# Column sums of phi(K) taken in the gram products, two row tiles turned by TensorE, and the whole program's order, engines and banks read from tables

## The chip, the cores and the metric

The kernel runs on one core of a Trainium2 chip. A time is the device time of one launch in microseconds (us); the time of a kernel is the median of its runs. The engines of the core are named as the profile names them: PE (TensorE, with PEld for its weight loads), DVE (VectorE), ACT (ScalarE), POOL (GpSimd) and SP (SyncE, which here only issues DMAs).

## The reference

Two kinds of layer alternate, each twice, on x of 2048 rows and 512 columns. The same weights serve both rounds.

```python
def _A_ref(x, wqkv, wo):          # H = 32 heads of 16
    q, k, v = split(x @ wqkv)
    phi = lambda t: jnp.where(t > 0, t + 1, jnp.exp(t)) + 1e-6
    pq, pk = phi(q), phi(k)
    kv = jnp.einsum("bhsd,bhse->bhde", pk, v)
    z = jnp.einsum("bhsd->bhd", pk)
    num = jnp.einsum("bhqd,bhde->bhqe", pq, kv)
    den = jnp.einsum("bhqd,bhd->bhq", pq, z)[..., None] + 1e-6
    return merge_heads(num / den) @ wo

def _B_ref(x, w1, w3, w2):        # F = 1792
    return (_silu(x @ w1) * (x @ w3)) @ w2

x = x + _A_ref(_layernorm(x), A_wqkv, A_wo)
x = x + _B_ref(_layernorm(x), B_w1, B_w3, B_w2)
x = x + _A_ref(_layernorm(x), A_wqkv, A_wo)
x = x + _B_ref(_layernorm(x), B_w1, B_w3, B_w2)
```

z is the sum of phi(K) over all 2048 rows, one number for each of the 512 columns.

## The kernel before

**Precision.** Each float32 operand of a product is scaled by a power of two and held as two float16 parts, high and low. A product takes three passes on PE: low by high, high by high, high by low (`PASSES`, L32; `mm`, L494). Splitting an operand costs a high part (a copy or a scaled copy to float16) and a low part (a subtraction, with two inputs).

**A pair of layers** is traced by `pair` (L1435): `attention` (L862), then `mlp` (L1444). `layer` 0 and 1 are the two rounds.

**Attention, keys.** The rows are cut into 16 tiles of 128. A tile is normalised (`keys_rows`), split into `nat` (two parts of 512 columns), turned by a DMA transpose into `xt` (`keys_turn`, L1107; the first three tiles by `ln_tile`, L484), and multiplied by the key weights: 12 matmuls of 512 columns into the PSUM tile `pk`. `phi_act` and `phi_sum` make phi(K), `high` and `low` (L914, L928) split it. `gram` (L878) adds nat-transposed times phi(K) into four banks `gt`, 12 matmuls a tile. The products with V's weights come later: `kv_products` multiplies the whole gram by them.

**Column sums before.** In layer 0 `gram_sum` (L870) multiplies both parts of phi(K) by a matrix of ones, two matmuls of 512 columns a tile, into the bank `pz`. In layer 1 POOL adds the tiles into `pksum` (L916 to L920), and `totals` (L953) sums over the partitions with one float32 matmul. Either way `pz` then holds z in every row, `inverse`, `keep_z`, `columns` (L981, eight float32 matmuls of one column) use it.

**Queries.** For each tile a product `pq` (`query`, L1148), phi, a denominator (`weigh_in`, `weigh_out`), a split and a DMA transpose, a product `po` with the combined weights `m_s`, and the sum into x (`attn_add`, L1209).

**MLP.** One level of a seven-product scheme: a group (`mlp_group`, L1287) has seven products P1 to P7 of 12 matmuls of 256 columns, for gate and up together, into the banks `ba`, `bb`, `bc`. ACT copies `bb` out between them (L1310), DVE adds `ba` and `bc` (L1313), then Silu on ACT (L1265), the product with up on DVE (L1266), the split of the hidden values (`hidden_parts`, L1268: high on ACT L1269, low on DVE or POOL L1271), four sums for the scheme (L1281 to L1284), and `mlp_out` (L1345, matmuls L1357; or `mlp_out_plain`, L1366) two groups later, into banks `po`. `mlp_add` (L1389) adds the banks into x. The columns of F come in seven groups in two or three sets, the rows in four chunks.

**Background in layer 0.** The MLP weights are loaded, bounded, split and stored while layer 0 runs: by `fill` inside attention and by `steps` inside the MLP.

**Order before.** Inside `in_order` (L257) each engine runs in the order in which the program is traced: the head and both attentions. The MLPs are ordered by the scheduler of the language, with `later` (L165) shifting priorities. PSUM is two pools of four banks, `acc` and `w`. Which engine takes a movable operation stands partly in the strings of `ENGINES` (L183; letter V is DVE, P is POOL, A is ACT), and partly in the code: normalising, the high parts of weights and hidden values, and the copies out of `bb` are always ACT's.

**Queues.** All DMAs go through SP in one queue, transposes too.

**Head.** 22 matmuls on ones keep PE busy, then the bound of the key weights, 10 more, the split of the key weights and the first three tiles.

Of the kernel before, what the change touches and what calls it, by code (L numbers as in the profile page):

```python
# [17 lines left out]
P = 128  # L18
# [9 lines left out]

SX = 2.0**9
PASSES = ((0, 0), (1, 0), (0, 1))  # L32

# [34 lines left out]
AT_JUNK = AT_T + 4 * KB  # L68
XB0, XB1 = AT_XB, AT_XB + 14 * KB


class Ring:
# [5 lines left out]
    def next(self, dtype, *dims):  # L78
        at = self.offsets[self.n % len(self.offsets)]
        self.n += 1  # L80
        return self.view(at, dtype, *dims)

# [6 lines left out]
def kernel(  # L89
# [15 lines left out]
    small = ctx.enter_context(tc.tile_pool(name="small", bufs=4))  # L105
    psum = ctx.enter_context(tc.tile_pool(name="psum", bufs=4, space=PSUM))
    dram = ctx.enter_context(tc.tile_pool(name="dram", bufs=1, space=DRAM))

    arena = const.tile([P, AT_END // 4], F32, name="arena")
# [17 lines left out]
    def acc_bank(name):  # L127
        return psum.tile([P, 512], F32, tag="acc", name=name)

    def bank(name):  # L130
        return psum.tile([P, 512], F32, tag="w", name=name)

    nats = (span(XB1 + 8 * KB, 3), span(AT_W2 + 2 * GROUP2, 3))
    nat_ring = Ring(view, *span(AT_NAT, 3), *nats[0])
# [30 lines left out]
    def later(n):  # L165

        return tc.high_priority(offset=-n)

    PINNED = ("PE", "DVE", "Activation", "Pool", "SP")
# [14 lines left out]
        (  # L184
            "plain:YYNN hid:VPVVVPVVVVVVVVPPVVVVVVVVVVVV den:AVVVVVVVVVVAVAAA "
            "bq:VAAA nat:PPAPAPPPAPPAAAAA key:PPPPPPAAPAAAAPPA "
            "norm:VVVPPPPPPPVVVVVV w13:PPPVVVV w2:PPVVPPP "
            "sums:VVVVVVVVVVVVVVVVVVPPPPPVPVVP rowsum:PPVVVVPP rowlow:PPVVVVVV "
            "keylow:PPPPPPPVVVPPPPPP natlow:PPPPPPPPPPPPPPPP "
            "add:PPPPPPVVVPPPVPPVPPPPVPVP"  # L190
        ),
        (
            "plain:NNNNNNNY hid:VVVVVVVVVVVVVVVVVVVVVVVVVVVV den:VVVVVVVVVVVVVVVV "
            "nat:AAAPPPPAPPPPPAAA key:AAAAAAPPAAAPPPAA "
            "norm:VVVPVVVPPVVVVVPP sums:VVVVVVVPVVVPPPPVVVVVVPVPVVVV "
            "rowsum:PPPPPPPP rowlow:PPPPPPPP keylow:PPPPPPPPPPPPPPPP "
            "natlow:PPPPPPPPPPPPPPPP add:PPPPPPPPPPPPPPPPPPPPPPPP"
        ),
# [57 lines left out]
    @contextmanager  # L256
    def in_order(*engines):  # L257

        traced = nc.cur_bb.bb.instructions
        before = traced[-1]  # L260
        depth.append(engines)
        yield
        depth.pop()
        if depth:
            return
        start = next(k for k in reversed(range(len(traced))) if traced[k] is before) + 1
        for i in traced[start:]:
            if str(i.engine).split(".")[-1] not in (engines or PINNED):
                continue
            if i.engine in pinned:  # L270
                tc.add_manual_dep(
                    i,
                    pinned[i.engine].name,
                    mybir.DependencyInfo(
                        mybir.DependencyClass.NoSync, mybir.DependencyReason.DATA
                    ),
                    reason="in_order",
                )
            pinned[i.engine] = i


    ident = view(AT_UV + 2 * KB, F32, P)
    make_identity(nc, ident)
    ones = const.tile([P, P], F32, name="ones")
    nc.vector.memset(ones, 1.0)
# [3 lines left out]
    make_block_diagonal(nc, mask, DH)  # L289
    scalars = const.tile([P, 42], F32, name="scalars")  # L290
    column = iter(range(38))

    columns_ = scalars[:, 38:42]
# [7 lines left out]
    nc.vector.memset(one_row[:1], 1.0)  # L301
    small_eps = scalar()
# [27 lines left out]
    st_w13 = view(AT_W + 42 * KB, F32, 2, 2, 2, F)  # L330
    raw2_ring = Ring(view, *span(AT_W + 28 * KB, 4))
# [55 lines left out]
    def split(hi, lo, src, scale):  # L387
        nc.scalar.activation(hi, src, AF.Copy, scale=scale)
        nc.vector.scalar_tensor_tensor(lo, src, scale, hi, OP.mult, OP.subtract)
# [8 lines left out]
    def engine_of(what, i):  # L398
        table = {what: table_of(what, state["layer"])}
        return {"V": nc.vector, "P": nc.gpsimd, "A": nc.scalar}[table[what][i]]  # L400
# [7 lines left out]
    def high_part(what, i, dst, src):  # L408
        engine = engine_of(what, i)
        if engine is nc.scalar:  # L410
            engine.activation(dst, src, AF.Copy)
        else:
            engine.tensor_copy(dst, src)

# [4 lines left out]
    def split_late(hi, lo, src, scale):  # L419

        nc.scalar.activation(hi, src, AF.Copy, scale=scale)  # L421
# [11 lines left out]
    def attn_bound(name, i):  # L433
        parts = small.tile([P, NK], F32, tag="parts", name="parts")
# [23 lines left out]
    def ln_moments(t0, n):  # L458
        for t in range(t0, t0 + n):
            st = small.tile([P, 6], F32, tag="st", name="st")  # L460
# [3 lines left out]
    def ln_scale(t0, n):  # L464

        ve = small.tile([P, n], F32, tag="ve", name="ve")
# [4 lines left out]
        neg = small.tile([P, n], F32, tag="neg", name="neg")  # L471
# [3 lines left out]
    def normalise(dst, t):  # L475
        nc.scalar.activation(  # L476
            dst,
            x_sb[:, t, :],
            AF.Identity,
            scale=rs_all[:, t : t + 1],  # L480
# [1248 lines left out]
```

## Time and profile before

| what | us |
|---|---|
| median of 3 runs | 1194.54 |
| lowest and highest run | 1193.79, 1195.58 |
| span of the profiled execution | 1192.4 |

The page gives no time of its own for the profiled execution beside its span; what lies around a span is taken as the median less the span, 2.1 us. The span runs from the first to the last instruction. A busy time is the sum of the durations of an engine's instructions with overlaps counted once; matmuls follow each other faster than one of them lasts, so the time of a matmul in a row is read from the distance of the starts. A line number is one of the kernel before. The row of the page with the DMA's share, in 40 slices of 29.8 us, shows where the queue is full:

```profile
DMA  8966665869632212111316434574342350120000
```

### The profile page before, as it was taken

What the parts mean: (1) busy time and instruction counts of PE and PEld (TensorE: products, weight loads), DVE (VectorE), ACT (ScalarE), POOL (GpSimd) and SP (SyncE); (2) the same over time, 40 slices, a digit from 0 to 9 for tenths busy, and PEclk for the clock granted to TensorE, in tenths of its full rate; (3) what the DMA queues carried; (4) which work ended last, traced back from release to release, by engine and by line L of the source; (5) the groups of instructions that cost most, each with busy time, mean ns of one, the idle gap of its engine ahead of it and who ended that gap; (6) DMA issues with size and microseconds to landing.
All of it is one profiled execution on the core that took longest, in us unless ns stands there. A gap on an engine that the chain in (4) does not pass through costs nothing.

```text
span 1192.4 us, 21837 instructions
## 1 busy us (share of the span) xinstructions
PE 1151.7 (97%) x8884; PEld 867.0 (73%) x8884; DVE 838.8 (70%) x1380; ACT 637.9 (53%) x1068; POOL 433.0 (36%) x500
## 2 busy tenths in 40 slices
PE   8999997899999999999999999998899999999998
PEld 3445444788888878888864454467788888888887
DVE  6888889767878887767785459757765654756443
ACT  6777687756545454434456644675544444444432
POOL 6452577212001121224358824774721122102010
PEclk9999999899999999999999999999999999999999
DMA  8966665869632212111316434574342350120000
GB/s 263 330 228 221 150 144 132 246 216 307 155 142 98 81 61 82 63 63 63 81 51 179 107 100 101 118 164 114 104 115 86 125 186 8 74 80 37 1 36 36
DMA packets 163396, 147.43 MB, mean 124 GB/s; under 512 B 129632, under 2 KB 138976, under 8 KB 158688
## 3 DMA queue, kind: packets, MB, share of 16 engines
q1 hardware_dynamic: 163296, 146.04, 42.1%
q8 instruction: 69, 1.13, 0.4%
q14 instruction: 31, 0.25, 0.1%
HBM read 72.48 MB, written 42.07 MB: 96 GB/s over the span
## 4 chain that ended last, share of the span: by engine, by line
PE 72%; DVE 13%; ACT 5%; DMA 5%; POOL 3%; issue 2%; SPq 1%; DVEq 0%; ACTq 0%; POOLq 0%
PE bb L499 18%; PE po L1357 14%; PE bc L499 9%; PE pq L499 6%; PE gt L499 5%; PE po L499 5%; PE pk L499 5%; PE ba L499 4%; PE po L1377 4%; DMA arena<-arena 3%; DVE arena L1266 2%; DMA arena<-in_B_w_dram 2%; DVE arena L1271 1%; DVE arena L1406 1%; ACT arena L1269 1%
## 5 line engine op out<-in xcount | busy, mean ns | idle before, releaser
L499 PEld LDWEIGHTS <-arena 128*128 128x128 f16 x6360 | 618.2, 98 | 260.9 <-issue 16.1
L499 PE MATMUL bb<-arena 128*128 128x256 f16 x2688 | 331.8, 273 | 7.4 <-ACT arena L1310 5.9
L1357 PE MATMUL po<-arena 128*128 128x256 f16 x1932 | 237.8, 274 | 11.5 <-ACT arena L1269 9.0
L1357 PEld LDWEIGHTS <-arena 128*128 128x128 f16 x1932 | 188.6, 98 | 37.5 <-ACT arena L1269 11.3
L1310 ACT ACTIVATE arena<-bb 128x512 f32<-128x512 f32 x196 | 115.2, 590 | 164.4 <-PE bb L499 135.2
L1271 DVE TENSOR_TENSOR arena<-arena 128x512 f16<-128x512 f32 (+1 forms) x108 | 123.9, 1148 | 96.8 <-ACT arena L1269 96.7
L499 PE MATMUL bc<-arena 128*128 128x256 f16 x1344 | 165.6, 273 | 1.6 <-DVE arena L1313 1.2
L1269 ACT ACTIVATE arena<-arena 128x512 f16<-128x512 f32 (+1 forms) x112 | 99.7, 891 | 95.7 <-DVE arena L1284 39.7
L1426 POOL TENSOR_TENSOR arena<-arena 128x512 f32<-128x512 f32 x28 | 40.4, 1442 | 286.1 <-DVE arena L1406 264.6
L1265 ACT ACTIVATE arena<-arena,scalars 128x512 f32<-128x512 f32 x112 | 74.7, 667 | 102.8 <-DVE arena L1313 100.7
L1266 DVE SCALAR_TENSOR_TENSOR arena<-arena,scalars 128x512 f32<-128x512 f32 x112 | 85.9, 767 | 52.8 <-ACT arena L1265 52.6
L1313 DVE TENSOR_TENSOR arena<-arena,bc 128x512 f32<-128x512 f32 x112 | 76.3, 682 | 50.3 <-ACT arena L1310 45.7
L1406 DVE SCALAR_TENSOR_TENSOR arena<-po,scalars,arena 128x256 f32<-128x256 f32 (+1 forms) x170 | 91.7, 583 | 14.0 <-PE po L1357 11.4
L499 PE MATMUL po<-arena 128*128 128x512 f16 x384 | 87.8, 379 | 4.1 <-DMA arena<-arena 2.8
L499 PE MATMUL pk<-arena 128*128 128x512 f16 x384 | 87.8, 379 | 2.8 <-DMA arena<-arena 2.8
L499 PE MATMUL gt<-arena 128*128 128x512 f16 x384 | 87.8, 379 | 1.6 <-ACT arena L915 1.0
L499 PE MATMUL pq<-arena 128*128 128x512 f16 x384 | 87.4, 379 | 0.9 <-DVE arena L1044 0.9
L499 PE MATMUL ba<-arena 128*128 128x256 f16 x672 | 86.3, 273 | 0.0
L476 ACT ACTIVATE arena<-arena,nb_all,rs_all 128x512 f32<-128x512 f32 x64 | 50.4, 808 | 32.3 <-POOL nb_all L473 28.3
L1377 PE MATMUL po<-arena 128*128 128x256 f16 x480 | 59.7, 280 | 3.4 <-ACT arena L1269 3.4
L423 DVE SCALAR_TENSOR_TENSOR arena<-arena,scalars 128x512 f16<-128x512 f32 (+2 forms) x60 | 50.3, 853 | 15.4 <-ACT arena L421 14.1
L1252 POOL TENSOR_TENSOR arena<-arena 128x512 f16<-128x512 f32 (+2 forms) x30 | 44.0, 1491 | 39.3 <-DMA arena<-arena 37.8
(164 smaller groups left out, 1258.3 us busy)
## 6 DMA issues: line engine op xcount, KB each, us to landing
arena<-xb_d SPq DMA_DIRECT2D x12, 1792.0 KB, 6.8
xb_d<-arena SPq DMA_DIRECT2D x8, 1792.0 KB, 5.9
xt_d<-arena SPq DMA_DIRECT2D x32, 256.0 KB, 2.5
arena<-xt_d SPq DMA_DIRECT2D x32, 256.0 KB, 3.1
arena<-in_B_w_dram SPq DMA_DIRECT2D x8, 896.0 KB, 7.2
arena<-in_B_w_dram SPq DMA_DIRECT2D x28, 256.0 KB, 4.1
w_d<-arena SPq DMA_DIRECT2D x4, 1792.0 KB, 9.5
arena<-w_d SPq DMA_DIRECT2D x4, 1792.0 KB, 6.8
```

What stands on the lines that cost most here:

```text
L423: lambda: nc.vector.scalar_tensor_tensor(lo, src, scale, hi, OP.mult, OP.subtract)
L476: nc.scalar.activation(dst, x_sb[:, t, :], AF.Identity, scale=rs_all[:, t : t + 1], bias=nb_all[:, t : t + 1],)
L499: nc.tensor.matmul(dst, lhs(a, k), rhs(b, k), start=first and k == 0 and i == 0, stop=last and k == n - 1 and i == len(PASSES) - 1, skip_g ...
L1265: nc.scalar.activation(t, gate, AF.Silu, scale=info["u1"])
L1266: nc.vector.scalar_tensor_tensor(t, up, info["hid"], t, OP.mult, OP.mult)
L1269: nc.scalar.activation(hs[:, 0, lo:hi], t[:, lo:hi], AF.Copy)
L1271: engine.tensor_tensor(hs[:, 1, lo:hi], t[:, lo:hi], hs[:, 0, lo:hi], OP.subtract)
L1310: nc.scalar.activation(dst, bank_, AF.Copy)
L1313: nc.vector.tensor_tensor(dst, dst, bank_, OP.add)
L1357: nc.tensor.matmul(po[:, i * HALF : (i + 1) * HALF], hs[:, a, qx, cs], w2[:, b, qw, :], start=g == ends[0] and i + a + b == 0, stop=g == e ...
L1377: nc.tensor.matmul(acc[n][:, half * HALF : (half + 1) * HALF], hs[:, a, qx, cs], w2_a21[g][:, b] if (i, half) == (0, 1) else w2[:, b, i + ...
L1406: nc.vector.scalar_tensor_tensor(dst, src, cb, to, OP.mult, OP.add)
```

## The change

1. **Column of ones.** `nat` of a key tile becomes 1026 columns: low part, high part, a one (`key_nat`, `set_ones`). The fourth of the four gram blocks takes its 128 stationary columns shifted by one, so that the last of them is the column of ones; its last row of `gt` is then z. The column of x that drops out (number 384) is replaced through the layer norm's zero row sum: row 384 of V's weights is subtracted from all of V's weights (`wv_row`, `prepare_vo`). `gram_sum`, the POOL additions of layer 1 and the matrix `ones` go. `totals` now copies the fourth bank and sums with `last_row` in both layers; `columns` has four matmuls for eight.
2. **First two tiles by TensorE.** `transpose_first`: eight matmuls with a float16 identity per tile into two banks, and two copies out.
3. **Tables.** `CHOICE` has one letter for each of 1247 movable operations (copies, scaled copies, normalising, subtractions and sums); `BANKS` one digit for each PSUM tile, 8 banks in one pool; `ORDER` the whole order of each engine and of SP by trace numbers, pinned by `pin_all`. `in_order`, `later` and the priorities go. `ORDER` has 8827 places for PE, 1506 for DVE, 915 for ACT, 448 for POOL and 326 for SP.
4. **Smaller ones.** `bring_table` loads ACT's function table ahead of the MLP and ahead of layer 1; 12 matmuls on ones at the start for 22; x's second tile is loaded after the key weights in the trace; small tiles in the arena.

```diff
-        def gram_sum(t):
-            if layer == 0:
-                pk = pks[t]
-                for a in range(2):
-                    nc.tensor.matmul(
-                        pz[0], ones16, pk[:, a, :], start=t + a == 0, stop=t + a == NT
-                    )
-
         def gram(t):
             pk, nat = pks.pop(t), nats.pop(t)
...
+            for j in (NK - 1, *range(NK - 1)):
+                at = j * P + (j == NK - 1)
+                for i, (a, b) in enumerate(PASSES):
+                    n = P - 1 if a == 1 and j == NK - 1 else P
+                    first = (1 - a) * D + at
+                    nc.tensor.matmul(
+                        gt[j][:n],
+                        nat[:, first : first + n],
+                        pk[:, b, :],
...
             def high():
-                nc.scalar.activation(pk[:, 0, :], e, AF.Copy, scale=info["tk"])
-                if layer == 1:
-                    if t == 0:
-                        nc.gpsimd.tensor_copy(pksum, e)
-                    else:
-                        nc.gpsimd.tensor_tensor(pksum, pksum, e, OP.add)
+                scale_to(pk[:, 0, :], e, info["tk"])
...
         def totals():
             held["rz"] = f32()
-            if layer == 1:
-                pz.append(bank("pz"))
-                nc.tensor.matmul(pz[0], ones, pksum, start=True, stop=True)
+            nc.scalar.activation(pksum, gt[NK - 1], AF.Copy)
+            pz.append(bank("pz"))
+            nc.tensor.matmul(
+                pz[0], last_row.to_broadcast([P, P]), pksum, start=True, stop=True
+            )
...
+    def transpose_first(xt, nat):
+
+        for a in (1, 0):
+            flipped = bank("flip")
+            for k in range(NK):
+                at = a * D + k * P
+                nc.tensor.matmul(
+                    flipped[:, k * P : (k + 1) * P],
+                    nat[:, at : at + P],
+                    ident16,
+                    start=True,
+                    stop=True,
+                )
+            to = xt[:, a * NK : (a + 1) * NK, :].rearrange("p k n -> p (k n)")
+            engine = choose()
...
+    def copy(dst, src):
+
+        engine = choose()
         if engine is nc.scalar:
             engine.activation(dst, src, AF.Copy)
         else:
             engine.tensor_copy(dst, src)
 
+    def scale_to(dst, src, scale):
+
+        engine = choose()
+        if engine is nc.scalar:
+            engine.activation(dst, src, AF.Copy, scale=scale)
+        else:
+            engine.tensor_scalar(dst, src, scale, None, op0=OP.mult)
+
+    def two(dst, a, b, op):
+
+        choose().tensor_tensor(dst, a, b, op)
...
     def hidden_parts(hs, t, lo, hi):
-        nc.scalar.activation(hs[:, 0, lo:hi], t[:, lo:hi], AF.Copy)
-        engine = nc.vector if lo else engine_of("hid", state["groups"])
-        engine.tensor_tensor(hs[:, 1, lo:hi], t[:, lo:hi], hs[:, 0, lo:hi], OP.subtract)
+        copy(hs[:, 0, lo:hi], t[:, lo:hi])
+        two(hs[:, 1, lo:hi], t[:, lo:hi], hs[:, 0, lo:hi], OP.subtract)
...
+        for before, i in zip(chain, chain[1:]):
+            tc.add_manual_dep(
+                i,
+                before.name,
+                mybir.DependencyInfo(
+                    mybir.DependencyClass.NoSync, mybir.DependencyReason.DATA
+                ),
+                reason="order",
+            )
...
+        "0-11 20 12-15 31-34 16-19 21-30 35-62 75-86 99-110 123-134 69-71 93-95 63-68 72-74 87-92 "
...
```

In this first line of PE's order the numbers are trace places: 0 to 11 and 21 to 30 are matmuls on ones, 20 is the one that spreads the bound, 12 to 19 and 31 to 38 turn tiles 0 and 1, 39 to 50 are the key product of tile 0, 51 to 62 of tile 1, 75 to 86 of tile 2, 99 to 110 of tile 3, 123 to 134 of tile 4, and 63 to 74 the gram of tile 0.

More of the change, by code (lines that the diff above doesn't have):

```diff
@@ L183 @@
     ENGINES = (
[L184 to L198, printed above, removed]
+        "plain:YYNN bq:VAAA den:AVVVVVVVVVVAVAAA norm:VVVPPPPPPPVVVVVV",
+        "plain:NNNNNNNY den:VVVVVVVVVVVVVVVV norm:VVVPVVVPPVVVVVPP",
     )
@@ L254 @@
     pinned, depth = {}, []
[L256 to L277, printed above, removed]
-                )
-            pinned[i.engine] = i
     ident = view(AT_UV + 2 * KB, F32, P)
     make_identity(nc, ident)
-    ones = const.tile([P, P], F32, name="ones")
-    nc.vector.memset(ones, 1.0)
+    ident16 = view(AT_UV + 2 * KB + 512, F16, P)
+    nc.vector.tensor_copy(ident16, ident)
     ones16 = const.tile([P, P], F16, name="ones16")
@@ L288 @@
     mask = const.tile([P, P], F16, name="mask")
[L289 to L293, printed above, removed]
+    nc.gpsimd.memset(mask, 0.0)
+    for base, compare in ((1 - DH, OP.is_gt), (0, OP.is_ge)):
+        nc.gpsimd.affine_select(
+            out=mask,
+            in_=mask,
+            compare_op=compare,
+            fill=(1.0, 0.0)[compare is OP.is_ge],
+            base=base,
+            pattern=[[-DH, P // DH], [0, DH]],
+            channel_multiplier=1,
+        )
+    scalars = const.tile([P, 44], F32, name="scalars")
+    column = iter(range(40))
+    columns_ = scalars[:, 40:44]
     def scalar():
@@ L433, in attn_bound @@
     def attn_bound(name, i):
-        parts = small.tile([P, NK], F32, tag="parts", name="parts")
+        parts = small("parts", NK)
         info[name] = parts
@@ L1308, in mlp_group, with take @@
         t = view(AT_T, F32, 7, HALF)
-        def copy(dst, bank_):
-            nc.scalar.activation(dst, bank_, AF.Copy)
+        def take(dst, bank_):
+            engine = choose()
+            if engine is nc.scalar:
+                engine.activation(dst, bank_, AF.Copy)
+            else:
+                engine.tensor_copy(dst, bank_)
         def add(dst, bank_):
@@ L1335, in mlp_group @@
             "o": lambda: middle(2),
-            "h": lambda: hidden(
-                engine_of("sums", state["groups"]), hs, t, late if "D" not in turn else None, plain
-            ),
+            "h": lambda: hidden(hs, t, late if "D" not in turn else None, plain),
             "e": lambda: middle(3),
@@ L1436, in pair @@
         state["layer"] = layer
[L1437 to L1441 removed]
+        attention(layer, ready, prep, before_gram)
         return mlp(layer, prep)
@@ L1475, in first_half @@
             if run["acc"] is None:
-                run["acc"] = [acc_bank(f"po{i}") for i in range(2 if run["plain"] else 4)]
+                run["acc"] = [bank(f"po{i}") for i in range(2 if run["plain"] else 4)]
             ready_for("plain" if run["plain"] else "w2", g)
@@ L1546, in mlp @@
                 if rows is not None:
-                    with later(far):
-                        for _ in range(ahead):
-                            next(rows, None)
+                    for _ in range(ahead):
+                        next(rows, None)
                 if layer == 0:
-                    with later(back):
-                        steps(more, budget)
+                    steps(more, budget)
                 if c == NC - 1:
@@ L1631, with first_tile @@
     ready = ({}, {})
-    def first_tile(t, engine=nc.gpsimd):
-        ready[0][t] = xk_ring.next(F16, 2 * NK, P)
-        ready[1][t] = ln_tile(t, ready[0][t], engine)
+    def first_tile(t):
+        keys_rows(t)
+        keys_turn(t, *ready, first=True)
+    first_banks = (0, 1)
     warm = bank("warm")
@@ L1695, with pin_all @@
     pair(1, nxt, None, second)
+    pin_all(nc, tc)
+def pin_all(nc, tc):
+    traced = {}
+    for i in nc.cur_bb.bb.instructions:
+        if str(i.opcode) not in ("RegisterMove", "TilePoolBoundary"):
+            traced.setdefault(str(i.engine).split(".")[-1], []).append(i)
+    for engine, runs in ORDER.items():
+        places = []
+        for run in runs.split():
+            first, _, end = run.partition("-")
+            places += range(int(first), int(end or first) + 1)
+        chain = [traced[engine][k] for k in places]
+        for before, i in zip(chain, chain[1:]):
[6 more added lines that the diff above has]
+                reason="order",
+            )
+ORDER = {
[146 rows of a table added]
+    ),
+    "DVE": (
[68 rows of a table added]
+    ),
+    "Activation": (
[38 rows of a table added]
+    ),
+    "Pool": (
[17 rows of a table added]
+    ),
[14 rows of a table added]
+    ),
+}
 _INS = ["A_x", "A_wqkv", "A_wo", "B_w1", "B_w3", "B_w2"]
```

432 lines of the change are left out of this document (224 added, 208 removed), and 282 rows, old and new, of the table ORDER.

## The prediction

> **What bounds the kernel now.** First the page's head and its row of engines.
>
> ```profile
> span 1192.4 us, 21837 instructions
> ...
> PE 1151.7 (97%) x8884; PEld 867.0 (73%) x8884; DVE 838.8 (70%) x1380; ACT 637.9 (53%) x1068; POOL 433.0 (36%) x500
> ```
>
> PE is the bound: only 40.7 us of the span are without a matmul. Whatever is gained is either PE work that goes or a part of those 40.7. The second view is the busy time by stretch (time, then PE, PEld, DVE, ACT, POOL, clock, DMA share, GB/s); I cut it where PE's idle time changes.
>
> ```profile
> 0.00:12.05 12.05, 9.10 (x35) 3.66 (x35) 7.57 (x24) 6.42 (x10) 7.62 (x23) 1.00 0.70 207
> 12.05:50.00 37.95, 34.63 (x157) 15.12 (x158) 27.00 (x48) 25.21 (x40) 19.84 (x37) 1.00 1.07 316
> 50.00:120.00 70.00, 70.00 (x375) 35.07 (x373) 58.35 (x116) 52.59 (x91) 28.11 (x40) 1.00 0.73 236
> 120.00:240.00 120.00, 108.19 (x609) 60.49 (x608) 104.97 (x193) 88.43 (x182) 71.48 (x74) 0.97 0.69 170
> ...
> 310.00:430.00 120.00, 112.54 (x1007) 98.80 (x1005) 102.67 (x169) 61.61 (x97) 14.08 (x13) 0.99 0.30 100
> 430.00:600.00 170.00, 170.00 (x1548) 151.23 (x1546) 124.55 (x202) 72.61 (x116) 51.64 (x53) 1.00 0.21 69
> 600.00:640.00 40.00, 37.22 (x239) 23.02 (x237) 27.08 (x41) 23.18 (x36) 28.91 (x36) 1.00 0.48 132
> 640.00:805.00 165.00, 164.68 (x871) 83.27 (x869) 105.78 (x187) 101.60 (x185) 104.22 (x129) 1.00 0.50 116
> 805.00:885.00 80.00, 71.76 (x641) 61.98 (x640) 57.00 (x72) 42.77 (x65) 40.65 (x34) 1.00 0.39 99
> 885.00:1192.40 307.40, 303.58 (x2781) 271.86 (x2779) 174.90 (x261) 123.24 (x185) 55.30 (x53) 1.00 0.20 71
> ```
>
> Time less PE gives the idle time by stage: head 3.0, loading 3.3, queries and first MLP groups of layer 0 11.8, the weight preparation 7.5, the change of layers 2.8, the first MLP chunk of layer 1 8.2, the tail 3.8. Elsewhere PE is full. Head and tail wait for the first load and the last store; 34.0 us lie between. Third, PE's waits:
>
> ```profile
> PE po L1357 <- ACT arena L1269: 9.0, 7, 2.9
> PE bb L499 <- ACT arena L1310: 5.9, 7, 2.1
> PE po L1377 <- ACT arena L1269: 3.4, 1, 3.4
> PE po L499 <- DMA arena<-arena: 2.8, 2, 2.1
> PE pk L499 <- DMA arena<-arena: 2.8, 4, 1.1
> ```
>
> The first three, 18.3 us, are one chain: bank copied by ACT, Silu, product, high part by ACT, then the matmuls that need it. A long wait costs twice, as PE's timeline shows:
>
> ```profile
> 227.62 5.09 PE L1377 MATMUL po<-arena 128*128 128x256 f16 x23 [3.42 <-ACT arena L1269]
> ...
> 246.69 3.00 PE L1377 MATMUL po<-arena 128*128 128x256 f16 x26
> ...
> 420.75 2.87 PE L1357 MATMUL po<-arena 128*128 128x256 f16 x13 [2.94 <-ACT arena L1269]
> ```
>
> At the usual pace (26 in 3.00 with the next start 2.84 later, so 0.109 each) 23 matmuls take 2.5; after the 3.4 us wait they took 5.1, and 13 took 2.9 for 1.4. That is 2.6 and 1.4 lost to the clock, whose mean in the stretch is 0.97.
>
> **The change part by part.** Prices of the PE work:
>
> ```profile
> 52.05 0.59 PE L874 MATMUL pz<-arena,ones 128*128 128x512 f16 x2
> 52.48 2.75 PE L499 MATMUL gt<-arena 128*128 128x512 f16 x12
> ```
>
> ```profile
> 699.00 1.02 PE L957 MATMUL pz<-arena,ones 128*128 128x512 f32 x2
> 699.86 7.93 PE L499 MATMUL pq<-arena 128*128 128x512 f16 x36
> 707.63 2.84 PE L499 MATMUL kv<-arena 128*128 128x128 f16 x48
> 710.31 1.90 PE L986 MATMUL pz<-scalars,arena 128*128 128x1 f32 x16
> 712.07 2.75 PE L499 MATMUL pq<-arena 128*128 128x512 f16 x12
> ```
>
> *Column sums.* Two matmuls move the next start by 0.43, so 0.215 each; 32 go: 6.9 us. The pair at 52.05 is the sixth; the ten of tiles 0 to 4 lie before 50 us, where the queue is full (DMA share 1.07) and PE waits for it anyway: those 2.2 may only turn into a wait. Bounds 4.7 and 6.9; I take the middle, 5.8. The gram keeps its matmuls and their columns; a shifted stationary block costs nothing.
>
> *Totals.* The float32 sum takes 0.86 (699.00 to 699.86); it is new in layer 0, and stays in layer 1. The one-column matmuls take 1.76 a layer and are halved: 0.9 gone twice. Net 0.9 gone. `totals` now waits for ACT's copy of the fourth bank (0.63, row L411 below). PE's table puts that block of the last tile, 416 to 418, ahead of nine others, 1.9 us, and the first query product: the cover. Without it 1.5 a layer would show.
>
> *First two tiles.* Sixteen matmuls of 128 columns at 0.056 (48 in 2.68): 0.9, put among matmuls on ones that do no work. Two transposes leave SP. What may be gained:
>
> ```profile
> 12.05 5.35 PE L499 MATMUL pk<-arena 128*128 128x512 f16 x24 [0.83 <-DMA arena<-arena]
> ```
>
> ```profile
> 10.05 2.56 ACT L388 ACTIVATE arena<-arena,scalars 128x512 f16<-128x512 f32 x4 [1.14 <-DVE scalars L373]
> ```
>
> The first key product waits 0.83 for a transpose; the weights' first high part is there at 10.7. So 0 to 1.4 us; I take 0.8. Two copies out of the flip banks a tile run on engines that also split the weights: if they are late, the term is zero. After that PE's table runs the key products of tiles 0 to 4 in a row before gram 0. It moves work within a stretch that the loads limit: 0, at worst 3 (the wait there today, once more).
>
> *DMA and SP.* Added: a broadcast row and one piece cut in two, some 0.25 MB against 147. [...] I take nothing.
>
> *Engines.* DVE has 1380 records, 32 of them reads of an accumulator, so 1348 against 1506 places: 158 more. ACT and POOL lose. The rows nearest to the new DVE operations:
>
> ```profile
> L1211 DVE DVE_READ_ACCUMULATOR arena<-po,scalars,arena 128x1 f32 x32 | 2.6, 82 | 0.0
> ...
> L373 DVE TENSOR_SCALAR arena<-pz 128x512 int32<-128x512 int32 x2 | 1.4, 686 | 4.0 <-PE pz L957 4.0
> ...
> L349 DVE TENSOR_SCALAR scalars<-scalars 128x1 int32<-128x1 int32 x8 | 1.2, 145 | 0.0
> ```
>
> ```profile
> L411 ACT ACTIVATE arena<-arena 128x512 f16<-128x512 f32 x30 | 18.9, 628 | 14.4 <-DVE arena L1188 9.2 <-POOL arena L1188 4.7
> ```
>
> No single-input DVE operation on 512 elements from SBUF stands in the trace. Above I bound it by 0.69 (L373, from PSUM), below by 0.15 (L349, one element); I take 0.69, the row of its size (ACT's copy, L411, takes 0.63). Over the program that is 109 us more on an engine that idles 354.
>
> [...]
>
> *Order.* This decides the size, and no row shows it. By stage: in 120 to 240 (11.8 idle, 2.6 of clock) DVE is 87% busy, ACT 74%, POOL 60%; part of the waits is load that an order can't remove, part is work spread unevenly over three engines: half, 7.2. In 310 to 430 (7.5 and 1.4) and 805 to 885 (8.2) ACT is near one half, POOL at 12% and 51%; PE waits for the length of a chain there, which other matmuls can cover: three quarters of 17.1, 12.8. In 600 to 640 half of 2.8, 1.4. Loading, head and tail: nothing.
>
> **The sum.** 5.8 + 0.9 + 0.8 + 7.2 + 12.8 + 1.4 = 28.9; 1192.4 less that is 1163.5. Runs lie 2.1 above a span (1194.54 less 1192.4): **1166 us**.
>
> **Rivals.** (a) *The order gives nothing*, only work goes: 7.5, so 1184.9 and 2.1: 1187. For it: PE is full already in 50 to 120 and 430 to 600. Against: 34 us of idle time between.
>
> (b) *The order gives all*: 30.7 idle (without loading), 4.0 of clock, 6.9, 0.9, 1.4: 43.9, so 1148.5 and 2.1: 1151. Against: DVE's load in 120 to 240.
>
> (c) *DVE becomes the bound of layer 0's queries and first groups*: slower. Of the first 200 letters of `CHOICE`, which cover about that attention (0 to 196 us), 52 are V; by the old strings and code about ten of these were DVE's (three of keylow, three of norm, low parts of the gram and the like). 42 more at 0.69 are 29 us, 120/196 of them 17.7 in the stretch 120 to 240. On DVE's 105.0 that is 122.7 of 120. If its 15 us of waits stay, the stage grows by 17.7: 1192.4 + 17.7 - 7.5 + 2.1 = 1205; the same rule in 310 to 430 (DVE 102.7 of 120) adds up to 8 more, 1213. It decides from the point where DVE's busy time there passes some 115 of 120, that is where an operation costs over 0.4. For it: DVE already 87% there. Against: ACT and POOL get room for what is on the chain.
>
> (d) *DVE and POOL slow each other.* The same operation, on the whole and before 622 us:
>
> ```profile
> L929 DVE SCALAR_TENSOR_TENSOR arena<-arena,scalars 128x512 f16<-128x512 f32 x32 | 30.5, 954 | 23.6 <-ACT arena L915 22.1 <-POOL arena L413 1.4
> ```
>
> ```profile
> L929 DVE SCALAR_TENSOR_TENSOR arena<-arena,scalars 128x512 f16<-128x512 f32 x17 | 13.8, 814 | 4.0 <-ACT arena L915 3.8
> ```
>
> The other 15, in layer 1 beside POOL's column sums, took 16.7/15 = 1.11: 0.30 more. Of the 158 new operations about 26 fall in 120 to 240; with POOL busy 60% of it, 26 x 0.6 x 0.30 = 4.7 us on a loaded engine: 1171. [...]
>
> (e) *The sums don't go*: excluded, as PE's table has no places for them.
>
> **Chances.** Forecast (1156 to 1180) 0.36, (d) 0.07, (a) 0.20, (b) 0.13, (c) 0.21, a mixture of gain and loss that ends near 1194.5 0.03. The range 1147 to 1210 leaves out the best end of (b) and the worst of (c), about 0.12. About 0.2% (2.4 us) is what a measurement of this kernel can tell: faster 0.36 + 0.07 + 0.13 + 0.17 of (a) = 0.73, same 0.06, slower 0.21.
>
> **What would show it.** PE: no pz sums, its work down by 7 to 8 us; idle time near 21 for 40.7, with few waits for the high part of hidden values. DVE: 850 to 950 us busy, and in 120 to 240 under 115. [...] The first key product before 12.0. Wrong: waits of PE on DVE in layer 0 above 15 us (c), waits for transposes in the first 60 us above 6, or idle time as before (a).

## The result, and the profile after

| | before | after |
|---|---|---|
| median, us | 1195.06 (1193.79 to 1195.69, 4 runs) | 1162.83 (1162.12 to 1165.21, 4 runs) |
| profiled span, us | 1192.4 | 1161.2 |
| time / time of before | | 0.9732, 95% interval 0.9714 to 0.975 |

The change makes the kernel 32.2 us faster; the forecast was 1166. The total came out, but not for the reasons given: one term was half again too small, and a cost that the prediction set at nothing was 9 to 11 us. First the head of the page of the changed kernel, with its row of engines.

```profile
span 1161.2 us, 21764 instructions
...
PE 1137.2 (98%) x8844; PEld 863.9 (74%) x8844; DVE 877.8 (76%) x1538; ACT 566.9 (49%) x970; POOL 365.6 (31%) x452
```

PE's records fall by 40 and its busy time by 14.5, twice the 7 to 8 that the prediction named as a sign; about 4 of that is the clock, and ten matmuls on ones fewer at the start make some 2.4. The idle time falls from 40.7 to 24.0. DVE has the 158 more instructions, and 39.0 us more of work, not the 109 that the prediction took. The busy time by stretch, with the cuts of the prediction, says where the idle time went.

```profile
0.00:12.05 12.05, 5.86 (x27) 3.18 (x28) 7.71 (x20) 5.36 (x7) 5.67 (x21) 0.93 0.82 295
12.05:50.00 37.95, 32.22 (x148) 14.21 (x145) 29.42 (x60) 20.42 (x32) 22.86 (x51) 0.95 1.06 254
50.00:120.00 70.00, 64.22 (x295) 30.48 (x296) 55.29 (x115) 41.00 (x72) 21.17 (x31) 0.94 0.79 225
120.00:240.00 120.00, 118.40 (x738) 69.89 (x736) 113.34 (x222) 91.67 (x190) 67.36 (x67) 1.00 0.64 153
310.00:430.00 120.00, 120.00 (x1101) 107.56 (x1100) 108.96 (x186) 56.63 (x90) 15.89 (x14) 1.00 0.41 151
600.00:640.00 40.00, 39.59 (x189) 18.45 (x188) 23.55 (x46) 19.20 (x30) 24.99 (x45) 1.00 0.61 163
805.00:885.00 80.00, 80.00 (x736) 71.70 (x734) 61.09 (x87) 37.75 (x59) 42.02 (x36) 1.00 0.39 111
```

Read the first two numbers behind the stretch, its length and PE's busy time, and the granted clock, third from the end. In the four stretches from 120 us on where PE had stood still before, the idle time falls from 11.8, 7.5, 2.8 and 8.2 to 1.6, 0, 0.4 and 0: 28.3 us gone, and the clock, 0.97 and 0.99 there before, is full, which gives some 4 us back. The first 120 us went the other way: idle 6.2, 5.7 and 5.8 where before it was 3.0, 3.3 and 0, at a clock of 0.93 to 0.95. That is 11.4 us of idle time more, and a slower pace. PE's waits name it.

```profile
PE bank L519 <- DMA arena<-arena: 12.7, 7, 9.6
PE bank L1663 <- DVE ones L257: 4.3, 1, 4.3
PE bank L344 <- DVE scalars L341: 1.9, 1, 1.9
```

All 18.3 us on ACT's copies and high parts are gone from this list. Nearly all that is left is in the head and in waits for DMA transposes, one of them of 9.6 us. PE's timeline (start, length, work, and in brackets the wait before it):

```profile
11.97 3.24 PE L1663 MATMUL bank<-ones 128*128 128x512 f16 x10
...
15.27 7.93 PE L519 MATMUL bank<-arena 128*128 128x512 f16 x36
...
54.51 4.57 PE L519 MATMUL bank<-arena 128*128 128x512 f16 x12 [9.57 <-DMA arena<-arena]
58.92 2.75 PE L897 MATMUL bank<-arena 128*128 128x512 f16 x12
```

The first key product starts at 15.27 us (12.05 before). The 9.57 us wait costs 1.8 more behind it: 12 matmuls take 4.57 there and 2.75 right after. To see what held the transposes, follow SP's queue backwards from 54 us (start and length of each issue, source line):

```profile
37.04 0.41 SPq L1624 DMA_DIRECT2D arena<-in_A_wqkv_dram  x1
37.50 5.25 SPq L1628 DMA_DIRECT2D arena<-in_A_wqkv_dram  x1
42.79 0.59 SPq L1628 DMA_DIRECT2D arena<-in_A_wo_dram  x1
43.43 0.60 SPq L1623 DMA_DIRECT2D arena<-in_A_wqkv_dram  x1
44.13 5.68 SPq L1112 DMA_TRANSPOSE arena<-arena  x1
```

A load's issue takes about half a microsecond here; the load right behind L1624 took 5.25 and the transpose, four issues later, 5.68, and the chain of work shows the transpose issued at 44.13 landing 10.33 later:

```profile
44.13 10.33 DMA arena<-arena
```

L1624 is new: it loads the last block of V's weights without its first row, 127 rows of 2 KB, 254 KB. The same view as above in stretches of 2 us, the last two columns being the share of the 16 DMA engines and GB/s:

```profile
40.00:42.00 2.00, 2.00 (x11) 0.91 (x10) 0.57 (x3) 1.78 (x3) 1.11 (x3) 1.00 0.06 17
...
48.00:50.00 2.00, 0.00 (x0) 0.00 (x0) 0.00 (x0) 0.00 (x0) 0.00 (x0) 0.50 0.07 26
50.00:52.00 2.00, 0.00 (x0) 0.00 (x0) 0.00 (x0) 0.00 (x0) 0.00 (x0) 0.50 0.06 25
```

A share of 0.06 is one engine of 16, at 25 GB/s; 254 KB at that rate are 10 us.

### The profile page after: what moved, and what is told of

Read it like the earlier page. It is cut to its first block, busy times and chain, and to the rows that moved or that the text cites. A ratio compares the mean times of both kernels' runs of the same rounds, so it can differ in the third digit from the quotient of the medians.

```text
span 1161.2 us, 21764 instructions
## 1 busy us (share of the span) xinstructions
PE 1137.2 (98%) x8844; PEld 863.9 (74%) x8844; DVE 877.8 (76%) x1538; ACT 566.9 (49%) x970; POOL 365.6 (31%) x452
## 4 chain that ended last, share of the span: by engine, by line
PE 80%; DVE 8%; DMA 4%; ACT 4%; issue 2%; POOL 2%; SPq 0%; POOLq 0%; DVEq 0%; ACTq 0%
PE bank L519 53%; PE bank L1373 18%; PE bank L897 6%; DMA arena<-arena 3%; PE bank L1393 3%; DVE arena L426 2%; POOL arena L426 1%; DVE arena L442 1%; DMA arena<-in_B_w_dram 1%; ACT arena L412 1%; DVE arena L1185 1%; DVE arena L373 1%; ACT arena L420 0%; ACT arena L1234 0%; DMA arena<-in_A_wqkv_dram 0%
## 5 line engine op out<-in xcount | busy, mean ns | idle before, releaser
L519 PE MATMUL bank<-arena 128*128 128x256 f16 (+1 forms) x5976 | 819.2, 293 | 14.0 <-DMA arena<-arena 12.7
L426 POOL TENSOR_TENSOR arena<-arena 128x256 f32<-128x256 f32 (+3 forms) x227 | 244.2, 1089 | 658.4 <-DVE arena L1422 167.3
L426 DVE TENSOR_TENSOR arena<-arena 128x256 f32<-128x256 f32 (+5 forms) x401 | 279.8, 719 | 44.4 <-ACT arena L412 26.1
L1373 PE MATMUL bank<-arena 128*128 128x256 f16 x1932 | 244.6, 273 | 0.0
L412 ACT ACTIVATE arena<-arena 128x512 f16<-128x512 f32 (+3 forms) x177 | 137.1, 786 | 106.7 <-DVE arena L426 35.8
L1326 ACT ACTIVATE arena<-bank 128x512 f32<-128x512 f32 x163 | 95.8, 594 | 181.1 <-PE bank L519 142.5
L1331 DVE TENSOR_TENSOR arena<-arena,bank 128x512 f32<-128x512 f32 x168 | 113.6, 681 | 70.5 <-ACT arena L1326 38.3
L1422 DVE SCALAR_TENSOR_TENSOR arena<-bank,scalars,arena 128x256 f32<-128x256 f32 (+1 forms) x170 | 95.4, 584 | 26.0 <-PE bank L1373 14.0
L1281 DVE SCALAR_TENSOR_TENSOR arena<-arena,scalars 128x512 f32<-128x512 f32 (+1 forms) x112 | 79.7, 713 | 36.9 <-ACT arena L1280 36.3
L897 PE MATMUL bank<-arena 128*128 128x512 f16 (+1 forms) x384 | 88.1, 379 | 0.0
L1393 PE MATMUL bank<-arena 128*128 128x256 f16 x480 | 58.3, 273 | 0.0
L877 DVE SCALAR_TENSOR_TENSOR arena<-arena 128x512 f32<-128x512 f32 x32 | 22.6, 716 | 32.3 <-ACT arena L867 28.3
```

Of the source, the lines that this page charges most:

```text
L426: choose().tensor_tensor(dst, a, b, op)
L519: nc.tensor.matmul(dst, lhs(a, k), rhs(b, k), start=first and k == 0 and i == 0, stop=last and k == n - 1 and i == len(PASSES) - 1, skip_g ...
L897: nc.tensor.matmul(gt[j][:n], nat[:, first : first + n], pk[:, b, :], start=t == 0 and i == 0, stop=t == NT - 1 and i == len(PASSES) - 1, ...
L1281: nc.vector.scalar_tensor_tensor(t, up, info["hid"], t, OP.mult, OP.mult)
L1326: engine.activation(dst, bank_, AF.Copy)
L1331: nc.vector.tensor_tensor(dst, dst, bank_, OP.add)
```

## The experiments

Each is compared with the kernel before, run on the same chip (medians 1193.73, 1194.15, 1193.9 and 1194.59 in the four groups); differences between the experiments are between medians. The kernel before had 1195.06 beside the changed kernel, so a difference of a microsecond between groups tells nothing.

### The 127 rows

`split112` loads the block in two pieces. The second piece gets a place in SP's order right behind the first.

```diff
-            nc.sync.dma_start(st_att[2][: P - 1, NK - 1, :], src[drop + 1 :])
+            nc.sync.dma_start(st_att[2][:112, NK - 1, :], src[drop + 1 : drop + 113])
+            nc.sync.dma_start(st_att[2][112 : P - 1, NK - 1, :], src[drop + 113 :])
```

> The changed kernel with the 127-row piece of V's weights loaded as 112 rows and 15 rows, nothing else. Theory A: that one piece (254 KB) runs on one of the 16 DMA engines, at some 25 GB/s, and everything behind it in the queue, a key tile's transpose too, waits; then the 9.57 us wait of PE at 44.9 to 54.5 us and the slow clock behind it (4.57 us for 12 matmuls that take 2.75) go: 9 to 12 us less, about 1152, and no stretch near 25 GB/s between 38 and 54 us. Rival B: the broadcast row (one row read 128 times) is the slow one; it stays, so the wait stays and the time is 1163. Rival C: the loads put ahead of the transposes in SP's order are at fault; then a wait of about 5 us or more remains near 45 us, and the time is 1157 or more.

Measured: 1153.81 us (1150.52 to 1154.05, 5 runs), ratio 0.9651 (0.9635 to 0.9668). That is 9.0 us below the changed kernel for 15 rows moved to a DMA of their own, and it is theory A; by the two rivals a long wait would have stayed. SP's queue and PE's waits in it:

```profile
39.22 0.45 SPq L1624 DMA_DIRECT2D arena<-in_A_wqkv_dram  x1
39.71 0.44 SPq L1625 DMA_DIRECT2D arena<-in_A_wqkv_dram  x1
...
41.62 1.24 SPq L1112 DMA_TRANSPOSE arena<-arena  x1
```

```profile
PE bank L519 <- DMA arena<-arena: 6.0, 6, 2.2
```

The transpose's issue takes 1.24 us for 5.68, and the wait of 9.6 us is gone. `split64` cuts the block at 64 rows instead:

> The same edit as split112, cut elsewhere: V's last piece of 127 rows is loaded as 64 and 63 rows instead of 112 and 15. Theory A (any number of rows that 16 doesn't divide goes through one engine): 63 rows, 126 KB, run at some 25 GB/s, about 5 us, a wait of 1 to 4 us near 54 us stays and the time lies 2 to 5 us above split112's, near 1156-1158. [...]

Measured: 1153.01 us (1150.97 to 1153.23), 0.9651 (0.9637 to 0.9664); from 36 to 54 us the stretches of 2 us show 202 to 383 GB/s. Theory A fails: 63 rows, which 16 does not divide either, are no trouble. One wait of 2.25 us for a transpose stays near 54 us, as theory A would have it, but in the stretches from 36 to 54 us the DMA share is 1.00 or more, not 0.06, and the time is that of `split112`. Of the pieces run here, of 127, 112, 64, 63 and 15 rows, the one of 127 alone was slow; why that count and not 63 is not shown.

### The head

`split_head` is `split112` with x's third tile behind the key weights, and the ones written first.

```diff
-    "SP":  "5 0 4 6 3 1-2 9 12 7 ...
+    "SP":  "5 0 4 3 1-2 6 9 12 7 ...
-    "DVE": "0 16 1 7 17 8 14 ...
+    "DVE": "1 0 16 7 17 8 14 ...
```

> The kernel of split112 with two entries of the tables moved: x's third row tile is loaded behind the last of the first key weights instead of ahead of three of them, and VectorE writes the ones (L257) ahead of the first statistics instead of behind them. Theory A: the first key product is late (14.4 us in split112, 15.3 in the changed kernel, 12.05 before) because the key weights stand behind x's third tile and the ones behind the statistics: the warm-up starts near 1 instead of 4.4, the first key product stands between 12.5 and 13.5, and the time falls by 0.8 to 1.8 us, to 1152-1153. Theory B: the stretch up to 120 us is set by the loads and their transposes, whatever TensorE starts with: the first key product is earlier all the same, but the waits for transposes (6.0 us together in split112) grow by as much, and the time stays within 0.5 us of split112's.

Measured: 1153.73 us (1153.4 to 1155.8), 0.9664 (0.9651 to 0.9677): no difference from `split112`. PE's timeline and its waits:

```profile
12.68 0.76 PE L344 MATMUL bank<-arena,scalars 128*128 128x128 f32 x2 [6.38 <-DVE scalars L341]
...
17.78 7.93 PE L519 MATMUL bank<-arena 128*128 128x512 f16 x36
```

```profile
PE bank L519 <- DMA arena<-arena: 2.9, 4, 1.3
```

Both theories had the first product earlier; it starts at 17.78, 3.4 us later than in `split112` (14.38). DVE's order is fixed as well, and there the statistics of the third tile (L480) stand ahead of the last three maxima of the key weights (L325); the tile now comes later, and these maxima wait behind it. Yet the time does not change, because the waits for transposes shrink from 6.0 to 2.9. So theory B holds in its main part: this stretch ends when loads and transposes let it, and 3 us at its start are covered.

### The first two tiles

`split_noflip` is `split112` with tiles 0 and 1 turned by DMA transposes; the 16 matmuls and two copies of each tile are left out.

```diff
-            transpose_first(xts[t], nat)
+            nc.sync.dma_start_transpose(xts[t], nat[:, : 2 * D])
```

> The kernel of split112 with the first two row tiles turned by DMA transposes as before (both issued behind the load of x's fourth tile), and the 32 flips by TensorE and their four copies out of the bank left out. Theory A (the prediction's term for the first two tiles, 0 to 1.4 us of gain): without the flips the first products wait for a DMA transpose, the first key product stands 0.5 to 2 us later than 14.4, and the time is 0 to 1.4 us above split112's. Theory B (the flips cost more than they bring, since the key weights are late anyhow and TensorE would else stand still): the first key product is not later, and the time is 0.3 to 1.5 us below split112's. Theory C: the transposes in the head get into the way of the loads behind them, and the time rises by more than 2 us.

Measured: 1155.78 us (1155.04 to 1156.31, 5 runs), 0.9677 (0.9664 to 0.9691): 2.0 us above `split112`. PE's timeline:

```profile
14.26 0.59 PE L519 MATMUL bank<-arena 128*128 128x512 f16 x2 [1.25 <-ACT arena L420]
...
20.52 5.56 PE L519 MATMUL bank<-arena 128*128 128x512 f16 x25 [3.31 <-DVE scalars L333]
27.95 2.76 PE L519 MATMUL bank<-arena 128*128 128x512 f16 x12 [1.88 <-DMA arena<-arena]
```

The ratios' intervals still touch, the times do not. The flips are worth some 2.0 us, more than the 0.8 of the prediction and its bound of 1.4. But not at the place it named: the first product is not later (14.26 against 14.38). The loss comes behind the first product, as a wait of 3.31 and one of 1.88. SP's queue shows where it starts:

```profile
10.21 2.72 SPq L1113 DMA_TRANSPOSE arena<-arena  x2
...
13.60 0.91 SPq L1621 DMA_DIRECT2D arena<-in_A_x_dram  x2
```

The two transposes stand ahead of two loads of x, which are issued at 13.60; in `split112` the same loads are issued at 6.70. DVE then idles 3.20 us for a tile of x, up to 18.92, and behind that tile's statistics its order has the last low part of the key weights (L373, 19.75 to 20.47; 16.58 in `split112`) and the small result (L333) that the wait of 3.31 is put down to. At the start of the gram the run is 2.1 us behind (33.56 against 31.43). So it is theory C's mechanism, at its limit of 2 us: the 2.0 is what two transposes cost at this place in the queue. Another place was not tried.

### The column sums

`nosum_before` is the kernel before, with the ones matmuls of the last tile alone: 30 of 32 are left out, and the column sums hold one tile.

```diff
-            if layer == 0:
+            if layer == 0 and t == NT - 1:
...
-                        pz[0], ones16, pk[:, a, :], start=t + a == 0, stop=t + a == NT
+                        pz[0], ones16, pk[:, a, :], start=a == 0, stop=a == 1
```

> The kernel before with 30 of the 32 matmuls on ones left out (the column sums of layer 0 then hold the last tile alone; the rest of the work is the same). The prediction's term: 30 x 0.215 = 6.5 us of PE work, of which 2.0 may turn into a wait for loads: 4.5 to 6.5 less, ratio 0.9946 to 0.9962. Rival: those matmuls are covered by waits for loads or for phi(K), and the time moves by less than 2 us.

Measured: 1189.69 us (1188.63 to 1190.65), 0.9962 (0.9949 to 0.9975): 4.0 us gained of the 6.45 that 30 matmuls took, between the prediction's term and the rival. Little of it lies where the matmuls went. PE's timeline:

```profile
19.13 0.59 PE L499 MATMUL gt<-arena 128*128 128x512 f16 x2 [1.88 <-ACT arena L915]
19.92 4.00 PE L499 MATMUL gt<-arena 128*128 128x512 f16 x10 [0.20 <-DVE arena L929]
...
105.66 7.98 PE L499 MATMUL pq<-arena 128*128 128x512 f16 x36
```

The first query product starts at 105.66 us, only 1.5 earlier than before (107.12). The first gram waits 1.88 for the high part of phi(K), where the ones matmul in front of it had waited 0.99, and the ten matmuls behind take 4.00, in a stretch (12.05 to 50 us) whose mean granted clock is 0.96; the ten matmuls on ones at 9.16, at a clock of 1.00, take 2.32. Near 99 us PE waits 1.72 for ACT (L848), a wait that was not there before. The other 2 to 2.5 us are gained later, where PE's waits on the high parts of hidden values (L1269) are 10.0 for 12.4; that the missing matmuls did this is not shown.

`backsums` is the opposite, in the new kernel: `split112` with two matmuls a tile put back into the gram of layer 0, by a stationary block of zeros.

```diff
+                    if layer == 0 and j == 0 and i == 1:
+                        for c in (0, 1):
+                            nc.tensor.matmul(gt[0][:64], zero16, pk[:, c, :], start=False, stop=False)
```

> The kernel of split112 with two matmuls of 512 columns a row tile put back into the gram of layer 0 (stationary block of zeros, so that the gram doesn't change): 32 matmuls, the work that the ones column took away. Theory A (the prediction's term): TensorE is the bound, each costs its 0.215 us, less the ten in the stretch that the loads limit: 4.7 to 6.9 us more, 1158.5-1160.7. Theory B (as where the 30 were left out of the kernel before: 4.0 us): 3.5 to 4.7 us. Theory C (the gram stretch of the new order waits for loads and transposes anyhow): under 2 us, in place of the waits for transposes before 60 us.

Measured: 1161.47 us (1160.4 to 1162.66, 5 runs), 0.9718 (0.9701 to 0.9734): 7.7 us above `split112`, more than any theory had. PE's timeline in `split112`, and then in `backsums`:

```profile
31.43 7.29 PE L897 MATMUL bank<-arena 128*128 128x512 f16 x33
38.55 2.75 PE L519 MATMUL bank<-arena 128*128 128x512 f16 x12
```

```profile
30.39 2.54 PE L899 MATMUL bank<-arena 128*128 128x512 f16 x11
32.86 0.62 PE L909 MATMUL bank<-arena,zero 128*64 128x512 f16 x2
...
39.48 2.75 PE L521 MATMUL bank<-arena 128*128 128x512 f16 x12
```

33 matmuls of the gram take 7.12 up to the next start in `split112`, and 9.09 here with three pairs among them: 0.66 a pair, not the 0.43 of the ones matmuls before. 16 pairs are 10.5. From the first gram matmul to the query products behind the one-column matmuls (31.43 to 108.44 in `split112`, 30.39 to 116.17 here) the stretch grows by 8.8; two waits for transposes in it, 0.28 and 1.09 in `split112`, are gone. The first gram starts 1.0 earlier, ahead of the first pair, and the edit does not explain that. So in the new order 7.7 to 8.8 of the 10.5 us show, in the old one 4.0 of 6.45, where other waits take the place of work that goes.

### The order

`nopins` is the changed kernel without the call of `pin_all`: engines and banks by the tables, the order as the framework makes it.

```diff
-    pin_all(nc, tc)
```

> The changed kernel without its pinned order: the same operations, engines and banks, ordered by the language's scheduler. Theory: the order is what removed PE's waits inside the program (30 us of idle time before, 2 after), so without it 30 us or more come back: 1190 or more. Rival: the engine letters and the eight free banks did it, and the time stays within 10 us of 1163.

Measured: 1272.27 us (1271.01 to 1272.43), 1.0651 (1.0636 to 1.0666): 109 us above the changed kernel and 79 above the kernel before. PE's waits:

```profile
PE bank L519 <- DMA arena<-arena: 23.9, 6, 13.7
PE bank L1373 <- ACT arena L412: 11.8, 6, 6.8
```

The theory's 1190 or more is met. The same choice of engines and banks, with the framework's order, ends far behind the kernel before, which had an order of its own in the head and in the attentions. What that choice is worth under a good order was not tried. Four more kernels, from `split112`, leave out one queue's table, or ScalarE's and GpSimd's together:

```diff
     for engine, runs in ORDER.items():
+        if engine in ("PE",):
+            continue
```

> The kernel of split112 with TensorE's table left out of the pinning: TensorE's instructions go in the order that the framework gives them, the other four engines keep theirs. Theory A (the gain is in the order of TensorE: which product stands between which, so that the engines behind it have the time they need): this gives up most of the 110 to 118 us that lie between no tables at all and split112, 60 or more, and TensorE's waits are on VectorE and ScalarE in the stages of the MLP. Theory B (TensorE's order follows from the others; the tables matter for the engines that feed it): 0 to 30 us.

> The same with VectorE's table alone left out. VectorE is at 114.8 of 120 us in the stage from 120 to 240 us. Theory A (so close to its limit, its order decides which hidden row tile comes in time): 15 to 60 us lost, most of it between 120 and 430 us. Theory B (TensorE's order leaves room enough): under 5 us.

> The same with SyncE's table alone left out: the order of loads, stores and DMA transposes is the framework's. The prediction took nothing for this order; the changed kernel with no tables at all waited 23.9 us for transposes. Theory A (the order of the queue is worth something after all): 8 to 30 us lost, as waits for DMA transposes in the first 120 us and wherever a store stands ahead of a load. Theory B (loads and transposes are hidden, as the prediction had it): within 2 us of split112.

> The same with ScalarE's and GpSimd's tables left out. Busy 567 and 368 of 1152 us, both have room. Theory A (an engine half empty needs no order): under 4 us lost. Theory B (ScalarE's evictions stand on the path to the next product, and its order decides when banks come free): 10 to 40 us lost, as waits on ScalarE's L412, L420 and L1326.

| left to the framework | median, us | ratio to before (95%) | above `split112` |
|---|---|---|---|
| TensorE | 1227.21 | 1.0277 (1.0262 to 1.0292) | 73.4 |
| VectorE | 1218.35 | 1.0209 (1.0186 to 1.0231) | 64.5 |
| ScalarE and GpSimd | 1214.96 | 1.0175 (1.016 to 1.019) | 61.2 |
| SyncE | 1192.19 | 0.9984 (0.9975 to 0.9994) | 38.4 |

TensorE meets theory A in size. The others lose more than any theory allowed: engines at half load or less lose 61 us, and SyncE's order alone 38. The place that theory A named for TensorE, waits on VectorE and ScalarE, is only a part: in all four runs the longest row of PE's waits is the one for DMA transposes, 22.9, 22.3, 29.8 and 28.8 us in the order of the table, against 6.0 in `split112`. Alone the losses add up to 237, together (`nopins`, against the changed kernel, both with the 127 rows whole) to 109. So these are not shares of the gain; they are what it costs to break one queue out of an order in which the others stay fixed. Two thirds of SyncE's loss are there by the end of layer 0's keys: the eight one-column matmuls start at 133.43 us, at 107.63 in `split112`. PE's timeline of that kernel, and then its queue of SP:

```profile
29.80 5.30 PE L519 MATMUL bank<-arena 128*128 128x512 f16 x12 [5.00 <-DMA arena<-arena]
51.30 7.81 PE L519 MATMUL bank<-arena 128*128 128x512 f16 x24 [16.19 <-DMA arena<-arena]
```

```profile
29.70 2.06 SPq L1629 DMA_DIRECT2D arena<-in_A_wo_dram  x4
...
37.87 8.19 SPq L1112 DMA_TRANSPOSE arena<-arena  x1
```

Four loads of the output product's weights and eight more transfers are issued ahead of a transpose; its issue takes 8.19 us, and PE's two waits for transposes make 21 us in the first 52. From 310 to 430 us and from 805 to 885 PE is full there; from 240 to 310 it idles 6.2 us, 0.2 in `split112`. So most of the MLP's gain doesn't hang on SP's order.

### VectorE's margin

`dveload` is the changed kernel with a reduction over 512 elements behind the residual sum of each row tile in layer 0, 16 in all, 0.686 each, between 147 and 224 us; nobody reads their results.

```diff
+        if state["layer"] == 0:
+            abs_max(spare[:, t : t + 1], x_sb[:, t, :])
```

> The changed kernel with one more reduction of 512 elements on DVE behind each of the 16 additions of layer 0's attention (0.68 us each, 10.9 in all, between about 125 and 220 us, where DVE is busy 113.3 of 120 us). Theory of the slower rival: at that load DVE is the bound of the stage, so 4 to 11 us are added, about 1167 to 1174, as waits of PE between 125 and 250. Rival: the order leaves slack behind DVE's operations, and less than 2 us are added.

Measured: 1170.69 us (1168.86 to 1171.55), 0.9801 (0.9786 to 0.9815): 7.9 us more for 11.0 us of work. In the stretch from 120 to 240 us PE's busy time falls from 118.40:

```profile
120.00:240.00 120.00, 114.12 (x668) 63.30 (x667) 114.29 (x228) 87.95 (x185) 65.66 (x66) 0.99 0.64 154
```

DVE's busy time there rises only from 113.34 to 114.29: the rest of its work is pushed later, and PE with it. The longest wait of PE there is one of 2.32 us for a transpose, behind which 12 matmuls take 4.45 us. Not all of the 7.9 is the added work: of the 8.6 us between the two profiled executions 2.1 lie ahead of the first added reduction (the query products start at 119.75 us, at 117.69 in the changed kernel). Some 6.5 us for 11.0 are left: VectorE has little room in this stage.

## Why the prediction was right in sum and wrong in its parts

**The order, 21.4 predicted.** The terms were half of the stage at 120 us, three quarters of the two MLP stages and half of the change of layers. The rows show 28.3 us of idle time and about 4.0 of clock gone: nearly all of it, which was rival (b). The waits that the prediction named are the ones that went; the size was off by 11. The shares were a choice without a row behind it, and the prediction held the load of the engines for a limit where it was none: DVE is at 113 of 120 us in the first of these stages, and PE still waits only 1.6. How much of it the order does, how much the work taken off ScalarE (busy 637.9 us before, 566.9 after), and how much the eight banks in one pool, stays open: `nopins` takes away the old order as well as the new one, so it shows only that engines and banks do not bring the gain under the framework's order. For the order speaks the stage from 310 to 430 us, where the other engines' load hardly moves (ACT 61.6 to 56.6, DVE 102.7 to 109.0, POOL 14.1 to 15.9) and all 7.5 us of waiting go; that is an argument, not a test.

**"DMA and SP: I take nothing."** This step failed. The "one piece cut in two" was weighed by its bytes, and it has 127 rows. It cost 9.0 us (`split112`), and 9.6 of the 11.4 us of idle time added in the first 120 us are this one wait. The head is 3.2 longer, but `split_head` shows that, without the 127 rows, some 3 us there are hidden. Two signs that the text named came out wrong, though the time was met: the first key product is not before 12.0, and the waits for transposes in the first 60 us are far above 6.

**So two errors cancel**: some 11 us more from the order and what came with it, some 11 us lost to loading. That the total was met is luck. Without the 127 rows the kernel takes 1153.8, near the 1151 of rival (b).

**Column sums, 5.8.** The shifted block costs nothing, as the prediction had it: the 12 gram matmuls of a tile move the next start by 2.59 in both kernels (104.53 to 107.12 us before, 58.92 to 61.51 after). The term itself: measured 4.0 in the old order (30 of 32), and 7.7 to 8.8 of 10.5 in the new one. At the same share the 6.9 of the ones matmuls would be 5.1 to 5.8 there, an estimate within the bounds 4.7 and 6.9. In the old order the lower bound failed, since removed PE work turned into waits outside the loading stretch too, and 1.5 us of gain is all that stands at its query products.

**First two tiles, 0.8.** Measured 2.0. The prediction named a wait of the first product for its transpose; the runs show loads of x that stand behind the transposes in SP's queue, and a loss behind the first product.

**Totals and columns, 0.9.** Not tried by itself. PE's list of waits has none on a copy of the fourth bank.

**VectorE.** Groups of the changed kernel by shape (instruction, shapes, count, then busy us and ns of one):

```profile
L414 DVE CAST arena<-arena 128x512 f16<-128x512 f32 x15 | 6.8, 455 | 1.9 <-PE bank L897 1.8
...
L503 DVE TENSOR_SCALAR arena<-arena,rs_all,nb_all 128x512 f32<-128x512 f32 x11 | 6.0, 548 | 0.0
L422 DVE TENSOR_SCALAR arena<-arena,scalars 128x512 f16<-128x512 f32 x8 | 3.8, 480 | 0.3 <-PE bank L897 0.3
...
L1328 DVE COPY arena<-bank 128x512 f32<-128x512 f32 x33 | 22.5, 685 | 4.1 <-PE bank L519 3.9
```

A copy or scaling from SBUF takes 0.455 to 0.548, between the prediction's bounds of 0.15 and 0.69, of which it took the upper; from PSUM it takes 0.685, the row of L373. The prediction took all 158 new operations for single-input ones of 512 elements. Counted by instruction they are 87 more sums and subtractions of two inputs (41 us), 32 copies out of PSUM (22 us) and 46 casts and scalings (21 us), with 6 fewer SCALAR_TENSOR_TENSOR (17 us less) and one MEMSET fewer. The durations grow by 67 us; the busy time, which counts overlaps once, by 39. Older work also becomes shorter, this one from 954 ns; GpSimd's sums, which stood beside it, are gone:

```profile
L936 DVE SCALAR_TENSOR_TENSOR arena<-arena,scalars 128x512 f16<-128x512 f32 x32 | 24.9, 785 | 10.8 <-ACT arena L420 9.0 <-POOL arena L422 1.2 <-POOL arena L512 0.5
```

**Rival (c)**, DVE as the bound of the stage at 120 us, did not come: DVE is busy 113.34 of 120 there, 8.4 more than before, not 17.7. But its point of decision, 115, was nearly met, and `dveload` shows that at this load the time grows by some 0.6 us for each microsecond of work. **Rival (d)** is not seen: the operation that named it became faster. **Rival (a)** is out, with 28.3 us of idle time gone.

## What to carry to other kernels

Before the bytes of a new DMA, look at its shape: here 127 rows in one piece ran at 25 GB/s, and in two pieces the kernel took 9.0 us less. In the profile look for a DMA share like the 0.06 here beside issues of several microseconds (5.25 and 5.68). The queues with a fixed order passed a delay on: the transpose four issues behind the 127 rows took 10.33 us to land, and PE waited 9.57; in `split_head`, with x's third tile loaded later and its statistics left at their place in VectorE's order, the first product came 3.4 us later. So move a load together with the instructions of the other queues that use it; leaving out one queue's table, or ScalarE's and GpSimd's, cost 38 to 73 us. And removed work was worth less than its full price: 4.0 of 6.45 us in the old order, where other waits took its place, 7.7 to 8.8 of 10.5 in the new one.

## What the runs showed of the hardware

- A DMA of 127 rows ran at 25 GB/s with a DMA share of 0.06, one engine of 16; cut in 112 and 15, or 64 and 63, the stretch from 40 to 52 us ran at 183 GB/s and more.
- In a wait of 9.57 us from 44.94 us on, the granted clock fell to one half (0.99 from 46 to 48 us, 0.50 from 48 to 52), and the 12 matmuls behind it took 4.57 us for 2.75. Waits near 2 us came out both ways: 12 matmuls took 4.37 behind one of 2.25 (`split64`) and 2.76 behind one of 2.19 (`split112`).
- GpSimd is far slower than DVE at a scaling with one factor a partition, 1.68 us against 0.48 for the same shapes, though its plain copy takes 0.69:

```profile
L422 POOL TENSOR_SCALAR arena<-arena,scalars 128x512 f16<-128x512 f32 x17 | 28.6, 1680 | 39.1 <-DVE scalars L357 28.1 <-DVE arena L877 10.0 <-DMA arena<-in_B_w_dram 0.9
L414 POOL CAST arena<-arena 128x512 f16<-128x512 f32 x27 | 18.6, 687 | 26.2 <-DVE arena L1281 7.7 <-DVE arena L1211 6.4 <-PE bank L897 5.4
```
